# Gated FFN with linear attention: the last chunk of the down projection by seven products, another order of the second half's chunks, and one weight split behind an elu

## The chip, the cores and the metric

The kernel runs on one core of one Trainium2 chip. The metric is the device time of one execution in microseconds (us), as the median of several runs. A profile of one execution gives, for each engine, which instruction ran when. The engines are PE (TensorE, the matmuls; PEld is its weight load), DVE (VectorE), ACT (ScalarE), POOL (GpSimd) and SP (SyncE, which issues all DMAs here). Each engine works through its own list of instructions in order, and an instruction waits at its head until what it needs is done.

## The reference

```python
def reference(A_x, A_wqkv, A_wo, B_x, B_w1, B_b1, B_w2, B_b2):
    def _A_ref(x, wqkv, wo):            # 32 heads of 18, S = 2048, D = 576
        ...
        phi = lambda t: jnp.where(t > 0, t + 1, jnp.exp(t)) + 1e-6
        pq, pk = phi(q), phi(k)
        kv = jnp.einsum("bhsd,bhse->bhde", pk, v)
        z = jnp.einsum("bhsd->bhd", pk)
        num = jnp.einsum("bhqd,bhde->bhqe", pq, kv)
        den = jnp.einsum("bhqd,bhd->bhq", pq, z)[..., None] + 1e-6
        o = num / den
        return (lambda x, *d: x.transpose(*d))(o, 0, 2, 1, 3).reshape(B, S, D) @ wo
    def _B_ref(x, w1, b1, w2, b2):      # F = 4608
        h = jnp.einsum("bsd,df->bsf", x, w1) + b1
        h = _gelu(h)
        return jnp.einsum("bsf,fd->bsd", h, w2) + b2
    x = A_x
    xn = _layernorm(x, axis=-1)
    s = _A_ref(xn, A_wqkv, A_wo)
    g = _silu(_B_ref(xn, B_w1, B_b1, B_w2, B_b2))
    return x + s * g
```

## The kernel before, in words

All arithmetic is fp32. A matmul operand is split into a high part (ACT rounds it, a CAST) and a low part (DVE subtracts the high part from the value); a product takes three matmuls, high·high, high·low and low·high. In the rows of the profile the names end in `_h` and `_l`, and line L837 is the high part (`set_hi`), L840 the low part (`set_lo`).

There are three stages. In the first (to about 145 us) 16 tiles of 128 tokens are normalized and give keys and values. In the second (to about 279 us) the loop `for i in range(1, NT + 4)` at L1108 projects the queries (`query`, L317), applies the elu (`phi`: three ACT steps L330, L332, L334 and one DVE step L336, which writes `phiq`), divides by the sums (`normalize`), transposes (`transpose_p`) and multiplies (`attend`, L813) with `kw`, the output weight folded with the attention state. `kw` has five parts. `split_kw(k)` makes the high and low halves of part k (ACT L359, DVE L360), and `attend(0)` is the first to use them, part 0 to part 4 in turn. The result s goes to `s_dram`.

The third stage is the FFN. It runs over two halves of 1024 tokens, and in each half over NC = 9 chunks of 512 hidden features: 18 chunks, `step` in the code. A chunk has two `Up` (each two blocks of 128 features times two blocks of 512 tokens, by seven products of sums of blocks instead of eight plain ones, L1189) and then the down projection, also by seven products (`product`, L1351), in the order `ORDER = (1, 2, 7, 4, 5, 3, 6)`. A down product has two halves (`q2`) of 12 matmuls of 128x288, each into a PSUM tile `pm`, and one DVE add (L1357) puts each half into the accumulators `macc`: C11, C12, C21, C22 (two blocks of tokens, b, times two halves of the output's columns, n) and U1, a sum that three of them share and that `combine` (L1367) adds at the end.

The down products need sums of the gelu's outputs `g`: POOL makes them (`HOps.S`: number 7 L1317, 5 L1308, 6 L1311, 3 L1314, each for the pair `pr` = 0 and 1 of the two `Up`), then come `hi` and `lo`. `W1` and `W2` are the weights' operands, made in the first half and stored to DRAM (`w1_dram`, `w2_dram`); in the second half they are loaded back. Chunk 8's W2 operands are not stored.

What stands where is written out by hand. A chunk has 28 steps: after each of the 14 up products (steps 0 to 13) and after each half of a down product (14 to 27) `at_step` emits what the tables `PH`, `PW2`, `W2_NEXT` and others put there. `in_order` then fixes the order on PE, DVE, ACT and POOL as it is emitted; the DMAs on SP are put in order by a scheduler.

The last chunk (`plain`, step 17) is different. Its down projection is done plainly: `down_plain` (L1451) takes eight tiles of 128 tokens one after the other, each with 24 matmuls of 128x288 (the last tile in two pieces of 384 and 192 columns). A tile ends with a DVE add of the accumulator (L1462), the silu on ACT (L1463), a DVE multiply with s (L1420), an add of x (L1421) and the DMA to `out` (L1422). The first half's output is finished in the course of the second half (`finish`, L1439 and L1440 on POOL).

Of the kernel before, what the change touches and what calls it, by code (L numbers as in the profile page):

```python
# [8 lines left out]
F32 = mybir.dt.float32  # L9
# [29 lines left out]
NWARM = 20  # L39

# [4 lines left out]
def linear_attention_gated_ffn(ctx, tc, x, xT, wqkv, wo, w1, w1e, b1, w2, b2, out):  # L45
# [78 lines left out]
    w1_dram, w2_dram = {}, {}  # L124

# [512 lines left out]
    def load_w2_raw(n):  # L638
        raw = w2rp.tile([P, 4, CF // 2, HD], F32, tag="w2raw", name=f"w2raw{n}")
        nc.sync.dma_start(raw.rearrange("p b a d -> p (b a d)"), w2[n % NC])  # L640
        return raw
# [207 lines left out]
    def load_we(n):  # L849
# [3 lines left out]
        g, q = divmod(n % NP, WG)  # L853
# [8 lines left out]
    class W1:  # L862


        def __init__(self, n):
            self.n = n
            raw = stage_w1(f"w1raw{n}")
            nc.sync.dma_start(raw, w1[n % NP])
# [43 lines left out]
    class W1Loaded(W1):  # L912


        def __init__(self, n):
            self.n, self.tiles = n, {}
            for i in ("a", "c", "d"):
                if i == "c":
                    t = w1r.tile([P, 8, P], F32R, tag="stw", name=f"wc_{n}")
                else:  # L920
                    t = w1_tile(i, n)
                self.tiles[i] = t
                nc.sync.dma_start(t.bitcast(F32), w1_dram[n % NP, i])

    def load_six(n):

        t = w1_tile("e", n)
        for k in range(2):
            six[n + k] = t[:, 4 * k : 4 * k + 4]
            nc.sync.dma_start(six[n + k].bitcast(F32), w1_dram[(n + k) % NP, 6])  # L930
# [177 lines left out]
    for i in range(1, NT + 4):  # L1108
# [25 lines left out]
        if 1 < i < NT:  # L1134
            phi_query(i)
        if 2 <= i < NT + 2:
# [3 lines left out]
        for k in {2: (0,), 3: (2, 4)}.get(i, ()):  # L1140
# [30 lines left out]
    class Up:  # L1171
        late = []

        def __init__(self, n, w, xs):
            self.p, self.w = n % NP, w
# [36 lines left out]
        def step(self, i):  # L1212
# [12 lines left out]
            elif i == 6:  # L1225
                self.mm(A, 6, first=False)
                nc.scalar.copy(u1_sb, A)  # L1227
                if self.p:
                    self.gelu(0, 0, B)
            elif i == 5:  # L1230
                self.mm(E, 5)
                nc.scalar.copy(m5_sb, E)
                if not self.p:
# [16 lines left out]
    class W2:  # L1250
# [21 lines left out]
        def plain(self, f):  # L1272
            k = 2 - 2 * (f % 2)
            self.src["p", f] = self.raw[:, k : k + 2, f // 2]

        def hi(self, i):
            tag = ORDER[i[1]] if isinstance(i, tuple) else i
            self.tiles[i], self.ops[i] = op_tile(fr, [2, HD], f"w2_{tag}", 1, f"w2_{self.n}_")
# [7 lines left out]
        def load(self, i):  # L1286
            t, self.ops[i] = op_tile(fr, [2, HD], f"w2_{i}", 1, f"w2_{self.n}_")
            nc.sync.dma_start(t.bitcast(F32), w2_dram[self.n % NC, i])

    class HOps:  # L1290
# [28 lines left out]
        def hi(self, i, pr):  # L1319
            self.ops[i, pr] = hi_lo(gp, [P, 512], f"h{HBUF[i, pr]}", 1, f"h{i}{pr}_")  # L1320
# [12 lines left out]
    }  # L1333
    ORDER = (1, 2, 7, 4, 5, 3, 6)
    CHAIN = {2: 1, 3: 5, 4: 7}
# [36 lines left out]
    tails = {}  # L1372

    def load_xs(t):
        F = lambda v: v.bitcast(F32)
        flat = lambda v: F(v).rearrange("p a b -> p (a b)")[:, :D]
        if t == 0:
            xt, s_t = flat(w1_tile("a", "x0")), stage_w1("s0")[:, :D]
        elif t == 1:
            xt = flat(w1_tile("a", "x1"))  # L1380
            s_t = flat(w1p.tile([P, WB, P], F32R, tag="we", name="s1", bufs=2))
        elif t == 2:
            xt, s_t = (flat(w1_tile("a", f"{v}2")) for v in "xs")
        elif t == 3:
            xt, s_t = stage_w1("x3")[:, :D], flat(w1_tile("a", "s3"))
        elif t == 4:
            raw = F(fr.tile([P, 2, D], F32R, tag="w2_5", name="xs4", bufs=1))
            xt, s_t = raw[:, 0], raw[:, 1]
        else:
            if t == 5:  # L1390
                tails["h"] = F(x_hi(2, "xs56")).rearrange("p a b -> p (a b)")
                tails["l"] = F(x_lo(2, "xs7")).rearrange("p a b -> p (a b)")
            v = {5: tails["h"], 6: tails["h"][:, 2 * D :], 7: tails["l"]}[t]
            xt, s_t = v[:, :D], v[:, D : 2 * D]
        nc.sync.dma_start(xt, x[t * P : (t + 1) * P, :])
        nc.sync.dma_start(s_t, s_dram[t])
        tails["xs", t] = xt, s_t

    def tail_split(b, f):
        src = h.A[f // 2, b, f % 2]  # L1400
        if b == 0:
            pair = hi_lo(gp, [P, 512], f"h{f}", 1, f"hp{f}_")
        else:
            k = f % 2
            if f < 2 and ("t", 0) not in tails:
                tails["t", 0] = x_lo(0, "hp0")
            if f >= 2 and ("t", 1) not in tails:
                tails["t", 1] = x_lo(1, "hp1")
            t = tails["t", f // 2]
            pair = t[:, 2 * k, :], t[:, 2 * k + 1, :]  # L1410
        set_hi(pair, src)
        tails["hs", b, f] = pair, src

    def tail_lo(b, f):
        pair, src = tails["hs", b, f]
        set_lo(pair, src, nc.vector)

    def gate(t, c, xt, s_t, cs=slice(0, D), eng=nc.vector):

        nc.vector.tensor_tensor(s_t[:, cs], c[:, cs], s_t[:, cs], op=MUL)  # L1420
        eng.tensor_tensor(s_t[:, cs], s_t[:, cs], xt[:, cs], op=ADD)  # L1421
        nc.sync.dma_start(out[t * P : (t + 1) * P, cs], s_t[:, cs])  # L1422


# [26 lines left out]
    def down_plain(t, ws):  # L1451

        bi, q = divmod(t, QH)
        cs = slice(q * P, (q + 1) * P)
        seq = []
        for f, (wh, wl) in enumerate(ws):
            hh, hl = tails["hs", bi, f][0]
            seq += [(hh, wh), (hh, wl), (hl, wh)]
        dst = c_tile(bi, q).rearrange("p n d -> p (n d)")

        def end(ps, c):
            nc.vector.tensor_tensor(c, ps, c, op=ADD)  # L1462
            nc.scalar.activation(c, c, AF.Silu)  # L1463

        def mm(ps, w, i):
            st, w_all = seq[i]
# [252 lines left out]
```

## Time and profile before

| | us |
|---|---|
| median of 3 runs | 1092.71 (1092.48 to 1092.85) |
| the profiled execution: time | 1092.45 |
| its span in the trace | 1090.6 |
| outside the span | 1.85 |
| PE busy | 1082.6 (99%) |
| DVE, ACT, POOL busy | 798.2, 549.2, 454.6 |
| down products of one chunk (PE) | 22.39 |
| plain down projection of the last chunk (PE) | 25.71, from 1060.17 |

The span is from the first to the last event on the core, and the time is measured around it. A row of the timeline reads: start, duration, engine, line, operation, output<-inputs, number of instructions, and in brackets how long the engine was idle before it and for whom.

### The profile page before, as it was taken

Reading aid. Unit: us, or ns where it says so; the run is one execution under the profiler, and the core shown is the slowest. Engines: PE = TensorE matmul, PEld = TensorE weight load, DVE = VectorE, ACT = ScalarE, POOL = GpSimd, SP = SyncE. Lnnn points to the kernel's source line nnn. Section 1 sums busy time; section 2 is a strip of 40 time slices with the busy share of each in tenths; the row PEclk is TensorE's granted clock in tenths of the full one; section 3 lists DMA queues with packets and bytes.
Section 4 is the critical chain, followed back from the end, with each engine's and each line's share of the span. In section 5 each row is a group of like instructions: output and inputs, shape, how many; then the busy total and the mean of one; then the engine's idle time right before and its main releaser. Section 6 shows DMA issues by size and latency. Waiting matters only on the chain.

```text
span 1090.6 us, 18119 instructions
## 1 busy us (share of the span) xinstructions
PE 1082.6 (99%) x6704; PEld 1007.4 (92%) x6704; DVE 798.2 (73%) x1099; ACT 549.2 (50%) x956; POOL 454.6 (42%) x391
## 2 busy tenths in 40 slices
PE   9999999999999999999999999999999999999998
PEld 8999999999898998988989989899898998988988
DVE  7776559888688898888988988657475574664856
ACT  6545476455646456465564654624335244252552
POOL 3555414332547455464555553414325143341340
PEclk9999999999999999999999999999999999999999
DMA  7999635675958659576595669968676666767452
GB/s 239 239 222 214 212 105 192 213 246 183 343 222 316 219 192 334 170 294 237 204 330 181 258 235 408 379 233 308 224 232 214 211 228 223 231 219 222 132 184 87
DMA packets 87266, 254.58 MB, mean 233 GB/s; under 512 B 11783, under 2 KB 24071, under 8 KB 84490
## 3 DMA queue, kind: packets, MB, share of 16 engines
q1 hardware_dynamic: 87178, 253.42, 69.7%
q8 instruction: 53, 0.87, 0.3%
q14 instruction: 35, 0.29, 0.1%
HBM read 156.57 MB, written 94.58 MB: 230 GB/s over the span
## 4 chain that ended last, share of the span: by engine, by line
PE 98%; DVE 1%; SPq 0%; ACT 0%; DMA 0%; issue 0%; POOL 0%; POOLq 0%
PE pm L1351 35%; PE a L1189 16%; PE bc L1189 10%; PE e L1189 10%; PE pk L317 6%; PE ps_s L813 5%; PE pq L317 5%; PE pv L317 4%; PE pd L1467 2%; PE ps_kva L378 1%; PE ptp L795 1%; PE warm L365 0%; PE ps_kw L728 0%; PE ps_kvb L378 0%; DMA wa_rest0q<-xh 0%; SPq L963 0%
## 5 line engine op out<-in xcount | busy, mean ns | idle before, releaser
L1357 DVE TENSOR_TENSOR macc<-pm,macc 128x576 f32<-128x576 f32 x218 | 164.4, 754 | 55.5 <-PE pm L1351 54.9
L837 ACT CAST h_h<-g 128x512 fp32r<-128x512 f32 x204 | 122.6, 620 | 132.2 <-PE pm L1351 131.6
L840 DVE TENSOR_TENSOR h_l<-g,h_h 128x512 fp32r<-128x512 f32 x204 | 154.6, 769 | 14.9 <-ACT h_h L837 13.9
L1317 POOL TENSOR_TENSOR mid<-g 128x512 f32<-128x512 f32 x34 | 44.0, 1293 | 134.9 <-ACT g L1205 134.9
L1218 ACT COPY mid<-a 128x512 f32<-128x512 f32 x36 | 21.1, 587 | 110.3 <-PE a L1189 110.1
L1224 DVE TENSOR_TENSOR bc<-bc,mid 128x512 f32<-128x512 f32 x36 | 25.1, 698 | 51.5 <-PE bc L1189 40.7
L1311 POOL TENSOR_TENSOR g<-g 128x512 f32<-128x512 f32 x34 | 52.2, 1535 | 20.8 <-ACT h_h L837 16.7
L883 POOL TENSOR_TENSOR w1raw<-w1raw 128x256 f32<-128x256 f32 x18 | 13.3, 737 | 113.9 <-ACT h_h L837 65.3
L1237 DVE TENSOR_TENSOR z<-a,mid 128x512 f32<-128x512 f32 x36 | 25.1, 698 | 46.6 <-PE a L1189 46.6
L1439 POOL TENSOR_TENSOR fin1l<-fin1h,fin1l 128x288 f32<-128x288 f32 x8 | 6.5, 808 | 122.8 <-DMA fin1l<-s_dram 57.9
L1314 POOL TENSOR_TENSOR g<-g 128x512 f32<-128x512 f32 x34 | 52.6, 1546 | 7.6 <-DVE h_l L840 5.5
L1308 POOL TENSOR_TENSOR g<-g 128x512 f32<-128x512 f32 x34 | 50.3, 1481 | 2.7
L778 POOL TENSOR_TENSOR pbuf<-phiq,den 128x576 f32<-128x576 f32 x16 | 19.0, 1188 | 61.2 <-DVE den L777 57.8
L1227 ACT COPY mid<-a 128x512 f32<-128x512 f32 x36 | 21.2, 588 | 44.3 <-PE a L1189 44.3
L1238 ACT COPY mid<-a 128x512 f32<-128x512 f32 x36 | 21.1, 587 | 40.0 <-DVE z L1237 40.0
L840 DVE TENSOR_TENSOR h_l<-mid,h_h 128x512 fp32r<-128x512 f32 x34 | 38.0, 1118 | 2.4 <-ACT h_h L837 2.4
L317 PE MATMUL pk<-wkv_h,xh 128*128 128x288 f32 (+1 forms) x160 | 38.2, 321 | 0.5 <-DVE xh L245 0.5
L317 PE MATMUL pk<-wkv_l,xh 128*128 128x288 f32 (+1 forms) x160 | 38.3, 322 | 0.1
L317 PE MATMUL pq<-wq_h,xh 128*128 128x288 f32 x160 | 34.7, 298 | 0.7 <-DVE phiq L336 0.7
L813 PE MATMUL ps_s<-kw_h,th 128*128 128x288 f32 x160 | 35.2, 302 | 0.0
L765 POOL TENSOR_TENSOR eq<-phiq,zb 128x576 f32<-128x576 f32 x16 | 22.9, 1432 | 27.6 <-DMA zb<-z_dram 19.4
L317 PE MATMUL pq<-wq_l,xh 128*128 128x288 f32 x160 | 34.3, 296 | 0.0
(891 smaller groups left out, 3709.0 us busy)
## 6 DMA issues: line engine op xcount, KB each, us to landing
we<-we_dram SPq DMA_DIRECT2D x36, 448.0 KB, 5.7
w2raw<-w SPq DMA_DIRECT2D x10, 1152.0 KB
w1raw<-w SPq DMA_DIRECT2D x18, 512.0 KB, 4.8
op_a<-wa SPq DMA_DIRECT2D x18, 512.0 KB, 4.6
op_c<-wc SPq DMA_DIRECT2D x18, 512.0 KB, 4.2
op_d<-wd SPq DMA_DIRECT2D x18, 512.0 KB, 2.7
wc<-op_c SPq DMA_DIRECT2D x18, 512.0 KB, 4.6
wa<-op_a SPq DMA_DIRECT2D x18, 512.0 KB, 5.0
```

What stands on the lines that cost most here:

```text
L317: nc.tensor.matmul(ps[:, h, : ws.stop - ws.start], st, w[:, k, ws], start=(begin and i == 0), stop=(end and i == len(seq) - 1), skip_group ...
L813: nc.tensor.matmul(ps[:, h, :HD], st[:, k, :], w[:, k, h * HD : (h + 1) * HD], start=(i == 0), stop=(i == len(seq) - 1),)
L837: nc.scalar.copy(pair[0], src)
L840: eng.tensor_tensor(pair[1], src, pair[0].bitcast(F32), op=SUB)
L1189: nc.tensor.matmul(ps, st, mv, start=first and n == 0, stop=n == len(seq) - 1, skip_group_check=True,)
L1224: tt(B, B, m1_sb, op=ADD)
L1308: tt(src[5, pr], A(1, 0), A(1, 1), op=ADD)
L1311: tt(src[6, pr], src[5, pr], A(0, 0), op=SUB)
L1314: tt(src[3, pr], A(0, 1), src[6, pr], op=SUB)
L1317: tt(src[7, pr], A(0, 0), A(1, 0), op=SUB)
L1351: nc.tensor.matmul(ps[:, q, :HD], hs[p][st][:, cs], m[:, p, :], start=(n == 0 and i not in CHAIN), stop=(n == 5), skip_group_check=True,)
L1357: nc.vector.tensor_tensor(dst, src, dst, op=ADD)
```

## The change

There are three parts.

1. **The last chunk.** `down_plain` and what belongs to it are gone. `last_chunk` does the seven products in the order `LAST = (1, 2, 5, 3, 6, 7, 4)`. Product 1 stays in the PSUM tiles `a0`, `a1`, and 6, 7 and 4 are added onto it there; product 2 goes to `e`, then 5, and 3 onto 5. After each half `drain` brings the accumulators in: after 2 the block C11 is final, after 6 C12, after 7 C22, after 4 C21. Each final block goes through `gate`: silu on ACT, multiply by s and add of x, then the DMA to `out`. For product 2 POOL does multiply and add; for 6, 7 and the first half of 4 DVE multiplies and POOL adds; the last half of 4 is done in two pieces of 128x288, multiply and add on DVE. The sums and splits of the operands stand in the table `PL`, their buffers in `HLAST`; the three `combine` stand at steps 1 to 3 instead of 4.
2. **The order of the second half's chunks.** They were taken 0 to 8; now `AGAIN` takes 8, 0, 1, ..., 7. The first one finds its W2 operands still in place, so the loads of W2 at the change of halves are gone; the last one (now chunk 7) loads its seven W2 operands like the others, where chunk 8's raw W2 was loaded and split before.
3. **The fifth split.** `split_kw(4)` moves from i = 3, between the splits 2 and 3, to i = 4, behind `phi_query(4)`.

The first place is DVE in the last chunk. The rows before are those of the plain tiles (`pd`; `xs`, `wa_s` and so on hold x and s):

```order
L1462 TENSOR_TENSOR macc<-pd_11579,macc 128x576
L1420 TENSOR_TENSOR xs_11327<-macc,xs_11327 128x576
L1421 TENSOR_TENSOR xs_11327<-xs_11327 128x576
L1462 TENSOR_TENSOR macc<-pd_11609,macc 128x576
L1420 TENSOR_TENSOR xs_11427<-macc,xs_11427 128x576
L1421 TENSOR_TENSOR xs_11427<-xs_11427 128x576
```

Now, from the first half of product 6 on (L1470 is the add in `drain`, L1442 the multiply by s, L847 the low part of an operand, L1474 the add of product 4):

```order
L1470 TENSOR_TENSOR e_11467<-a_11431,macc 128x2x288
L1442 TENSOR_TENSOR gated_11366<-e_11467,gated_11366 128x2x288
L847 TENSOR_TENSOR h_l<-g,h_h 128x512
L1470 TENSOR_TENSOR e_11468<-a_11432,macc 128x288
L1470 TENSOR_TENSOR e_11468<-a_11433,macc 128x288
L1442 TENSOR_TENSOR gated_11382<-e_11468,gated_11382 128x2x288
L1470 TENSOR_TENSOR e_11467<-a_11431,macc 128x2x288
L1442 TENSOR_TENSOR gated_11428<-e_11467,gated_11428 128x2x288
```

Each multiply stands between the add of its own half and the add of the next; the silu between them is on ACT.

The second place is ACT at the end of the last `Up`. Before, after the last gelu come the last splits and then only silus:

```order
L1205 ACTIVATE g<-bc_11345,b1c 128x512
L837 CAST hp_11454<-g 128x512 x2
L1463 ACT_TABLE_LOAD
L1463 ACTIVATE macc<-macc 128x576 x7
L1463 ACTIVATE macc<-macc 128x384
```

Now (L1440 is the silu, L844 a high part; `h_x_11487` are the operands 5 and 3 of pair 1):

```order
L1214 ACTIVATE g<-bc_11324,b1c 128x512
L844 CAST wa_h_11425<-g 128x512
L1440 ACT_TABLE_LOAD
L1440 ACTIVATE macc<-macc 128x2x288
L844 CAST h_x_11487<-g 128x512
L1440 ACTIVATE macc<-macc 128x2x288
L844 CAST h_x_11507<-mid 128x512
L844 CAST h_x_11487<-g 128x512
```

The high parts of the operands 5 and 3 (pair 1) stand behind the silus of product 2's two halves; on POOL the sum for operand 3 stands likewise behind the multiply and add of product 2's first half.

The third place is DVE around the elu of tile 4. Before (`kr_1804`, `kr_1840`, `kr_1822` are the parts 2, 4 and 3):

```order
L360 TENSOR_TENSOR kw_l<-kr_1804,kw_h 128x576
L360 TENSOR_TENSOR kw_l<-kr_1840,kw_h 128x576
L360 TENSOR_TENSOR kw_l<-kr_1822,kw_h 128x576
L773 TENSOR_REDUCE den_1943<-eq_1911 128x32
L776 TENSOR_SCALAR den_1943<-den_1943 128x32
L777 RECIPROCAL den_1943<-den_1943 128x32
L336 SCALAR_TENSOR_TENSOR phiq_1982<-pq_1948,eq_1978 128x576
```

Now:

```order
L367 TENSOR_TENSOR kw_l<-kr_1804,kw_h 128x576
L367 TENSOR_TENSOR kw_l<-kr_1822,kw_h 128x576
L780 TENSOR_REDUCE den_1941<-eq_1911 128x32
L783 TENSOR_SCALAR den_1941<-den_1941 128x32
L784 RECIPROCAL den_1941<-den_1941 128x32
L343 SCALAR_TENSOR_TENSOR phiq_1980<-pq_1946,eq_1976 128x576
L367 TENSOR_TENSOR kw_l<-kr_1840,kw_h 128x576
```

Part 4 of `kw_l` now follows `phiq`; on ACT its high part follows the elu's third step in the same way.

The diff, cut to its core:

```diff
+AGAIN = (NC - 1, *range(NC - 1))
...
+    def chunk_of(step):
+        return step if step < NC else AGAIN[step - NC]
+
+    def pair_of(n):
+        return 2 * chunk_of(n // 2) + n % 2
...
-                nc.sync.dma_start(t.bitcast(F32), w1_dram[n % NP, i])
+                nc.sync.dma_start(t.bitcast(F32), w1_dram[pair_of(n), i])
...
+        if i == 4:
+            split_kw(4, nc.vector)
...
-        for k in {2: (0,), 3: (2, 4)}.get(i, ()):
+        for k in {2: (0,), 3: (2,)}.get(i, ()):
             split_kw(k, nc.vector)
...
-            nc.sync.dma_start(t.bitcast(F32), w2_dram[self.n % NC, i])
+            nc.sync.dma_start(t.bitcast(F32), w2_dram[chunk_of(self.n), i])
...
+    HLAST = {
+        (1, 0): 0, (1, 1): 1, (2, 0): 2, (2, 1): 3, (6, 0): 4, (4, 1): 0, (5, 0): "w", (3, 0): "w",
+        (5, 1): (0, 0), (3, 1): (0, 2), (6, 1): (1, 0), (7, 1): (1, 2), (7, 0): (3, 0), (4, 0): (3, 2),
+    }
+    LAST = (1, 2, 5, 3, 6, 7, 4)
...
+    def load_gated(k):
+        flat = x_hi((0, 2, 1, 3)[k], f"gated{k}").bitcast(F32).rearrange("p a b -> p (a b)")
+        xt, st = (flat[:, v : v + 2 * D].rearrange("p (q d) -> p q d", q=2) for v in (0, 2 * D))
...
+    def last_chunk(hops, ws, base):
+        a0 = bank2("a0")[:, :, :HD]
+        a1 = [bank1(f"a1{q}")[:, :HD] for q in range(2)]
+        e = []
+        tt = nc.vector.tensor_tensor
+        def gate(b, n, q2, c, q=slice(0, 2), eng=(nc.vector, nc.gpsimd), last=False):
+            cs = slice(n * HD, (n + 1) * HD)
+            xt, st = (v[:, q, cs] for v in gated[2 * b + q2 // 2])
             nc.scalar.activation(c, c, AF.Silu)
+            to = c if last else st
+            eng[0].tensor_tensor(to, c, st, op=MUL)
+            eng[1].tensor_tensor(st, to, xt, op=ADD)
...
+        def drain(i, q2):
...
+            if i == 1:
+                for a, c, _ in banks(C11):
+                    tt(c, a, c, op=ADD)
+            elif i in (2, 5, 3):
+                c = macc[:, q2 : q2 + 2, {2: C11, 5: C22, 3: C12}[i], :]
+                tt(c, ps, c, op=ADD)
+                if i == 2:
+                    gate(0, 0, q2, c, eng=(nc.gpsimd, nc.gpsimd))
+            elif i in (6, 7):
+                for a, c, to in banks({6: C12, 7: C22}[i]):
+                    tt(to, a, c, op=ADD)
+                gate(int(i == 7), 1, q2, ps)
+            else:
+                for q, (a, c, _) in enumerate(banks(C21)):
+                    tt(a, a, c, op=ADD)
+                    if q2:
+                        gate(1, 0, q2, a, q=q, eng=(nc.vector, nc.vector), last=True)
+                    else:
+                        gate(1, 0, q2, a)
+        for k, i in enumerate(LAST):
...
+            for q2 in (0, 2):
...
+                        nc.tensor.matmul(
+                            ps, hs[p][st][:, cs], m[:, p, :], start=n == 0 and i in (1, 2, 5),
...
+                drain(i, q2)
+                at_step(base + 14 + 2 * k + q2 // 2)
...
+    PL = dict(
+        S={(7, 0): 7, (5, 0): 8, (6, 0): 9, (3, 0): 10, (7, 1): 13, (5, 1): 14, (6, 1): 15, (3, 1): 16},
+        hi={
+            (1, 0): 7, (2, 0): 8, (5, 0): 9, (6, 0): 10, (1, 1): 11, (2, 1): 12, (3, 0): 13,
+            (5, 1): 16, (7, 0): 17, (3, 1): 18, (6, 1): 19, (7, 1): 20, (4, 0): 21, (4, 1): 22,
+        },
...
+            if change:
+                w2t[step + 1] = w2t[step]
+            else:
                 make(W2, w2t, step + 1)
                 for i, at in W2_NEXT.items():
-                    add(base + at + 10 * change, lambda i=i, n=step + 1: w2t[n].load(i))
...
+                    add(base + at, lambda i=i, n=step + 1: w2t[n].load(i))
...
+            for k, m in enumerate((C12, C21, C22)):
+                add(base + 1 + k, combine, m, nc.gpsimd)
+            for k, at in enumerate((9, 10, 13, 14)):
+                add(base + at, load_gated, k)
...
-    for t in range(2 * QH):
-        down_plain(t, ws)
```

More of the change, by code (lines that the diff above doesn't have):

```diff
@@ L1227, in step @@
                 nc.scalar.copy(u1_sb, A)
-                if self.p:
+                if not self.first:
                     self.gelu(0, 0, B)
@@ L1232, in step @@
                 nc.scalar.copy(m5_sb, E)
-                if not self.p:
+                if self.first:
                     self.gelu(0, 0, B)
@@ L1370, in c_tile @@
         return macc[:, q, 2 * bi : 2 * bi + 2, :]
[L1372 to L1422, printed above, removed]
     def silu_first(s):
@@ L1624, in linear_attention_gated_ffn @@
                     add(base + 26 + k, combine, C21, nc.gpsimd, slice(2 * k, 2 * k + 2))
-            for what in ("S", "hi", "lo"):
-                for (i, pr), at in PH[what].items():
-                    add(base + at, getattr(h, what), i, pr)
+        for what in ("S", "hi", "lo"):
+            for (i, pr), at in (PL if plain else PH)[what].items():
+                add(base + at, getattr(h, what), i, pr)
         if half == 1 and c == 0:
@@ L1660, in linear_attention_gated_ffn @@
         if plain:
+            last_chunk(h.ops, w2t[step].ops, base)
             break
```

121 lines of the change are left out of this document (55 added, 66 removed).

## The prediction

> **What bounds the kernel now.** I read the page first, then the chain of waits in order of time, then PE's own waits, and only then the timeline of the end.
>
> ```profile
> span 1090.6 us, 18119 instructions
> PE 1082.6 (99%) x6704; PEld 1007.4 (92%) x6704; DVE 798.2 (73%) x1099; ACT 549.2 (50%) x956; POOL 454.6 (42%) x391
> ```
>
> ```profile
> 1015.53 22.39 PE pm L1351 x168
> 1037.91 1.62 PE a L1189 x7
> 1060.17 25.71 PE pd L1467 x192
> ```
>
> ```profile
> PE warm L365 <- POOL ident masks.py:199: 2.0, 1, 2.0
> PE pq L317 <- DVE phiq L336: 0.7, 1, 0.7
> PE pk L317 <- DVE xh L245: 0.5, 1, 0.5
> ```
>
> PE is the bound, and it waits for 3.2 us in the whole span. So a change can gain in three ways: fewer matmuls, PE's last wait (0.7 us for `phiq`), or what follows the last matmul. A down projection by seven products takes 22.39 us of PE for 168 matmuls, so 1.60 us for a half of 12; the last, plain one takes 25.71. A chunk is 44.64 us (1015.53 to 1060.17), and none of the waits lies in the FFN, the change of halves included. The end of the program, on DVE and on ACT:
>
> ```profile
> 1082.51 0.76 DVE L1462 TENSOR_TENSOR macc<-pd,macc 128x576 f32<-128x576 f32 x1
> 1084.01 0.76 DVE L1420 TENSOR_TENSOR xs<-macc,xs 128x576 f32<-128x576 f32 x1 [0.75 <-ACT macc L1463]
> 1084.69 0.55 DVE L1462 TENSOR_TENSOR macc<-pd,macc 128x384 f32<-128x384 f32 x1
> ```
>
> ```profile
> 1087.63 0.36 DVE L1421 TENSOR_TENSOR xs<-xs 128x192 f32<-128x192 f32 x1
> ```
>
> ```profile
> 1083.30 0.68 ACT L1463 ACTIVATE macc<-macc 128x576 f32<-128x576 f32 x1 [2.49 <-DVE macc L1462]
> 1085.27 0.53 ACT L1463 ACTIVATE macc<-macc 128x384 f32<-128x384 f32 x1 [1.29 <-DVE macc L1462]
> 1086.30 0.36 ACT L1463 ACTIVATE macc<-macc 128x192 f32<-128x192 f32 x1 [0.49 <-DVE macc L1462]
> ```
>
> Two things are to be seen. PE's matmuls end at 1085.88, DVE's last add at 1087.99, and the output's DMA takes the other 2.6 us to 1090.6. And one round on DVE, add, wait of 0.75 for the silu, multiply, takes 2.18 us from the start of an add (1082.51) to the start of the next instruction behind the multiply (1084.69). Plain tiles come every 3.2 us, so the round fits under PE.
>
> **Part 1, the last chunk.** On PE it removes 25.71 us and adds 22.39: a gain of 3.3 us if PE doesn't wait and the tail stays as it is. Neither holds, because the outputs become final in the last three products, every 1.60 us, and DVE has a round of 2.18 for each. DVE is in order, and each multiply stands ahead of the next half's add. The rows for the walk, of DVE, ACT and POOL in the last chunk and of groups over the span:
>
> ```profile
> 1060.31 0.69 DVE L1242 TENSOR_TENSOR bc<-bc,mid 128x512 f32<-128x512 f32 x1
> 1061.05 0.69 DVE L840 TENSOR_TENSOR hp_l<-g,hp_h 128x512 fp32r<-128x512 f32 x1
> ```
>
> ```profile
> 1061.04 0.69 ACT L1205 ACTIVATE g<-bc,b1c 128x512 f32<-128x512 f32 x1
> ...
> 1062.77 1.28 ACT L1463 ACT_TABLE_LOAD   x1
> ```
>
> ```profile
> 1045.56 7.96 POOL L1367 TENSOR_TENSOR macc<-macc 128x1152 f32<-128x1152 f32 x3
> 1084.90 1.41 POOL L1421 TENSOR_TENSOR xs<-xs 128x576 f32<-128x576 f32 x1 [31.38 <-DVE xs L1420]
> ```
>
> ```profile
> L837 ACT CAST h_h<-g 128x512 fp32r<-128x512 f32 x204 | 122.6, 620 | 132.2 <-PE pm L1351 131.6
> L840 DVE TENSOR_TENSOR h_l<-g,h_h 128x512 fp32r<-128x512 f32 x204 | 154.6, 769 | 14.9 <-ACT h_h L837 13.9
> L1317 POOL TENSOR_TENSOR mid<-g 128x512 f32<-128x512 f32 x34 | 44.0, 1293 | 134.9 <-ACT g L1205 134.9
> L1308 POOL TENSOR_TENSOR g<-g 128x512 f32<-128x512 f32 x34 | 50.3, 1481 | 2.7
> L330 ACT ACTIVATE eq<-pq 128x576 f32<-128x576 f32 x16 | 10.4, 652 | 34.3 <-PE pq L317 34.3
> ```
>
> The `combine`s (8 us of POOL) move ahead of `finish` and end near 1046.7; the first sum waits for a gelu four us later, so this costs nothing. Product 1 starts at 1060.17 as the plain one did. The last gelu ends at 1061.73, and POOL's sums for pair 1 (1.29, then 1.48 to 1.5 each) end at 1063.0, 1064.5 and 1066.0. Product 2's first half ends at 1060.17 + 3 x 1.60 = 1064.97. Then come the add (to 1065.77), the silu (0.69, to 1066.50; the table load fits in before), the cast of operand 5 that stands behind it (to 1067.05) and its low part on DVE (0.69, to 1067.78). Product 5 starts at 1066.57 and needs that low part with its sixth matmul at 1067.24: PE waits 0.57.
>
> Next on DVE are product 2's second add (to 1068.46) and the low part of operand 7, whose cast stands behind the second silu: 1069.78 to 1070.46. The add of product 5's first half comes only after it, to 1071.15. Product 3 accumulates onto the same tile and would have started at 1070.34: PE waits 0.85. On POOL the multiply and add of product 2's first half (1.41 each, from 1066.54) push the sum for operand 3 to 1070.8; cast and low part end at 1072.2, and the sixth matmul of product 3 wants them at 1071.86: 0.38 more. So PE loses 1.80 us, and product 6's first half ends at 1060.17 + 9 x 1.60 + 1.80 = 1076.37.
>
> From there DVE is the bound. Three rounds with one add take 0.80 + 0.69 + 0.69 = 2.18 each. (The silu now reads PSUM: 0.65, as the relu from PSUM in L330.) Two rounds whose add is in two 288-column pieces (0.455 each, between the 0.36 of 192 columns and the 0.55 of 384) take 2.25. With the low part of operand 4 in between (0.61) that is 11.65 us, against 8.0 of PE for the same five halves; PE now waits for DVE, since product 4 accumulates onto the tile that product 7's add must have read. The last two pieces, each add, silu, multiply and add in turn on 288 columns (0.45 + 0.04 + 0.41 + 0.04 + 0.45 + 0.03 + 0.38 = 1.80), do not overlap on DVE: 3.60 us. DVE ends at 1076.41 + 11.65 + 3.60 + 0.07 = 1091.73, that is 3.74 later than the 1087.99 of before. SP's last stores wait in order behind POOL's add for product 4's first half, which ends near 1089.6 and so holds nothing. The last DMA has 144 KB instead of 96; I add 0.1 us.
>
> [...]
>
> Bounds. The PE waits are worth at most -1.8 us if all vanish. POOL at 1.33 for 576 columns (half of one of L1367's 1152-column adds) or at 1.67 (L1308's 1.48 for 512 columns, scaled) instead of 1.41 moves the end by -0.2 or +0.6, in the same walk. Low parts at their mean of 0.77 instead of 0.69, which is with other engines at work, add 0.2, and rows longer still up to 1. Rounds 0.12 shorter (add and multiply at the 0.69 of the 512-column add L1242) take 0.6 off. Loads of x and s (eight before, four pairs now) start when the x operands are last read, 1052 to 1060, and the first is wanted at 1066.5; a 288 KB load took 3.2 us (row below), so this has cover of several us.
>
> **Part 2, the chunks' order.** PE waits nowhere around the change of halves, and each operand is loaded most of a chunk ahead of its use, so I cost it at 0. Seven loads of W2 go from SP's queue at the change of halves and come back before the last chunk, where other chunks have them too. One thing is new: the load of a W1 operand now needs a store that stands just ahead of it.
>
> ```profile
> 636.48 0.32 SPq L834 DMA_DIRECT2D op_c<-wc  x1
> 637.75 0.32 SPq L834 DMA_DIRECT2D op_d<-wd  x1
> 638.16 0.41 SPq L923 DMA_DIRECT2D wc<-op_c  x1
> 639.61 0.32 SPq L834 DMA_DIRECT2D op_a<-wa  x1
> 643.15 0.32 SPq L834 DMA_DIRECT2D op<-w  x1
> ```
>
> ```profile
> op_c<-wc SPq DMA_DIRECT2D x18, 512.0 KB, 4.2
> ```
>
> ```profile
> wa_x<-x SPq DMA_DIRECT2D x2, 288.0 KB, 3.2
> ```
>
> With 4.2 us for such a store to land, SP would stand until about 641 at that load, and the store after it be 1 to 2 us late; by the next one at 643.15 SP has caught up. The operand is wanted tens of us later. Bounds: 0 to +3.
>
> **Part 3, the fifth split.**
>
> ```profile
> 173.74 0.43 PE L813 MATMUL ps_s<-kw_l,th 128*128 128x288 f32 x2
> 174.88 0.53 PE L317 MATMUL pq<-wq_h,xh 128*128 128x288 f32 x2 [0.71 <-DVE phiq L336]
> ```
>
> ```profile
> 172.73 0.78 ACT L334 ACTIVATE eq<-eq,tiny 128x576 f32<-128x576 f32 x1
> ```
>
> ```profile
> L360 DVE TENSOR_TENSOR kw_l<-kr,kw_h x4: 695/746/1117, 167.7 to 172.0; 128x576 fp32r<-128x576 f32 x4
> ```
>
> ```profile
> 174.07 0.76 DVE L336 SCALAR_TENSOR_TENSOR phiq<-pq,eq 128x576 f32<-128x576 f32 x1
> ```
>
> Without one split ahead of it `phiq` starts about 0.7 us earlier, 173.36 to 174.12, and the 0.71 us that PE waited are gone. But `attend(0)` ends with the fifth part, and PE wants its low half at 173.74. It now comes behind `phiq`: 174.12 to 174.80. Its two matmuls (0.27) start at 174.84, and the next query at 175.11 instead of 174.88: +0.2. Ends: -0.71 if nothing takes the wait's place, +0.6 with the longest of the split's rows (1.12).
>
> **Sum.** 3.74 + 0.1 + 0 + 0.2 = +4.05 on 1092.45, the profiled execution: 1096.5. The median of the runs is 0.26 above that execution, so 1096.8.
>
> **Rivals.** (B) DVE keeps pace and PE stays the bound: the products end at 1060.17 + 22.39 = 1082.56, and with 2.7 us of DVE tail and 2.7 of DMA the span is 1088.0, 2.6 less: 1090.1. For it speaks that PE really has 3.3 us less to do; it decides if a round gets under 1.60 us, which needs the 0.75 of waiting for the silu out of DVE's list. The order of the rows forbids it. (C) The early waits vanish, because sums and splits come in time; then DVE's rounds start at 1074.6 and the end is 1.8 earlier: 1095.0. Against it, DVE has little free between 1069.8 and 1076 in the walk. (D) POOL and low parts go at their slow values, all rounds start a microsecond or two later: 1098.2. (E) The split's part does what it takes away, -0.7 instead of +0.2: 1095.9, inside the range. (F) The W1 load holds PE at the change of halves: 1099.8 at its end of +3; PE's cover speaks against it.
>
> **How the numbers follow.** About 0.2% (2.2 us) is what a measurement of this kernel can tell from no change. Chances: the forecast with E 0.60 (1095.5 to 1098), C 0.15, D 0.17, B 0.04, F 0.04. Slower by over 2.2 us means over 1094.9: the forecast, D and F nearly whole and half of C, 0.85. Within 2.2: 0.11, the rest of C and the forecast's low corner, where C and E and shorter rounds meet. Faster: 0.04, B. The range 1094.2 to 1098.9 leaves out B, F and the edge of D.
>
> **What would show it.** In the profile after: PE's products from 1060.4 on with waits of about 0.6 before the sixth matmul of product 5, about 0.9 and 0.4 at product 3, and then waits on DVE at products 7 and 4; DVE adds from product 6 on 2.2 us apart with a wait of about 0.7 on ACT ahead of each multiply; about 6 us from the last matmul to DVE's last add, instead of 2.1; chunks at 44.64 us across the change of halves; PE's wait near 174 us now on `kw_l`, not `phiq`. I am wrong if PE ends later than DVE's list lets me think (rounds under 1.7 us), or if the DVE rounds begin before 1075.

## The result, and the profile after

The changed kernel takes 1099.35 us (median of 4 runs, 1098.81 to 1099.44) where the kernel before takes 1092.70 (4 runs): a ratio of 1.006, 95% interval 1.0043 to 1.0077. That is 6.65 us slower. I had forecast slower, by 4.1 us, with 1098.9 as the upper end of the range, so the direction was right and the size was not. The profiled execution after took 1098.81 us, its span is 1097.1 (before 1092.45 and 1090.6).

The head of the page and PE's waits after (columns of the second fence: who waited for whom, total us, times, the longest):

```profile
span 1097.1 us, 18090 instructions
PE 1080.7 (99%) x6680; PEld 1003.9 (92%) x6680; DVE 798.3 (73%) x1102; ACT 549.4 (50%) x958; POOL 480.8 (44%) x407
```

```profile
PE ps_s L820 <- DVE kw_l L367: 1.3, 1, 1.3
PE e L1494 <- DVE h_x L847: 1.2, 2, 1.0
PE a L1494 <- DVE e L1470: 1.0, 1, 1.0
PE e L1494 <- DVE macc L1465: 1.0, 1, 1.0
```

PE works 1.9 us less and waits 4.5 us at places where it waited 0.7 before. The chain of waits puts the last full chunk here:

```profile
1016.42 22.39 PE pm L1371 x168
```

With 44.64 us for a chunk the last one starts at 1061.06 (before 1060.17). Its DVE, from the low part of operand 5 (pair 1) on, with the places that the prediction walked through:

```profile
1067.90 1.50 DVE L847 TENSOR_TENSOR h_x<-g,h_x 128x512 fp32r<-128x512 f32 x1 [1.26 <-ACT h_x L844]
1069.32 0.74 DVE L1465 TENSOR_TENSOR macc<-e,macc 128x576 f32<-128x576 f32 x1
1071.33 1.15 DVE L847 TENSOR_TENSOR h_x<-mid,h_x 128x512 fp32r<-128x512 f32 x1 [1.26 <-ACT h_x L844]
1072.41 0.74 DVE L1465 TENSOR_TENSOR macc<-e,macc 128x576 f32<-128x576 f32 x1
1073.07 1.23 DVE L847 TENSOR_TENSOR h_x<-g,h_x 128x512 fp32r<-128x512 f32 x1
...
1074.89 1.24 DVE L847 TENSOR_TENSOR h_x<-g,h_x 128x512 fp32r<-128x512 f32 x1
...
1076.73 0.67 DVE L847 TENSOR_TENSOR h_x<-mid,h_x 128x512 fp32r<-128x512 f32 x1
...
1078.76 0.77 DVE L1470 TENSOR_TENSOR e<-a,macc 128x576 f32<-128x576 f32 x1
1080.23 0.76 DVE L1442 TENSOR_TENSOR gated<-e,gated 128x576 f32<-128x576 f32 x1 [0.70 <-ACT e L1440]
...
1090.64 0.46 DVE L1474 TENSOR_TENSOR a<-a,macc 128x288 f32<-128x288 f32 x1
...
1093.84 0.46 DVE L1443 TENSOR_TENSOR gated<-a,gated 128x288 f32<-128x288 f32 x1
```

Two things are to be seen. The DVE rounds begin at 1078.76, 17.70 us after the chunk's start, and the forecast's walk has 16.24. And a low part (L847) takes 0.67 in one row and 1.15 to 1.50 in four others of the same shape, while the adds between them, which read PSUM, keep to 0.74 to 0.77. The four long rows are the low parts of operands 5 (pair 1), 7 (pair 0), 3 and 6 (pair 1). POOL in that stretch:

```profile
1067.44 1.41 POOL L1442 TENSOR_TENSOR gated<-macc,gated 128x576 f32<-128x576 f32 x1 [0.47 <-ACT macc L1440]
1068.93 1.75 POOL L1443 TENSOR_TENSOR gated<-gated 128x576 f32<-128x576 f32 x1
1070.64 1.29 POOL L1318 TENSOR_TENSOR g<-g 128x512 f32<-128x512 f32 x1
1071.89 1.87 POOL L1442 TENSOR_TENSOR gated<-macc,gated 128x576 f32<-128x576 f32 x1
1073.83 1.76 POOL L1443 TENSOR_TENSOR gated<-gated 128x576 f32<-128x576 f32 x1
```

Put the ends side by side. POOL's operations end at 1068.85, 1071.93, 1073.76 and 1075.59; the four long low parts end at 1069.40, 1072.48, 1074.30 and 1076.13: 0.55, 0.55, 0.54 and 0.54 later. So these low parts, begun while POOL worked, were not slowed a little, they stood until POOL's operation was over. In turn POOL's 1.75 at 1068.93 ends 1.28 after the low part that was running (1069.40). So the two took turns.

The whole difference in spans, term by term (measured by rows shown here or in the next section):

| term | forecast | measured |
|---|---|---|
| fifth split | +0.2 | +0.76 |
| order of the chunks | 0 | 0 |
| last chunk's start to the first round on DVE | 16.24 | 17.70 |
| five rounds with one low part (1078.76 to 1090.64) | 11.65 | 11.88 |
| last two pieces (1090.64 to 1094.30) | 3.67 | 3.66 |
| DVE's end to the span's end | 2.7 | 2.8 |

The misses are 0.56, 1.46, 0.23 and 0.1; with 0.13 by which the last chunk starts later beyond the split (+0.89 against +0.76) they make the 2.5 us between +4.05 and +6.5. What makes the 0.13 was not tried; the order of the chunks does not (see its run below).

### The profile page after: what moved, and what is told of

It is laid out like the page before. It is cut to its first block, busy times and chain, and to the rows that moved or that the text cites. A ratio compares the mean times of both kernels' runs of the same rounds, so it can differ in the third digit from the quotient of the medians.

```text
span 1097.1 us, 18090 instructions
## 1 busy us (share of the span) xinstructions
PE 1080.7 (99%) x6680; PEld 1003.9 (92%) x6680; DVE 798.3 (73%) x1102; ACT 549.4 (50%) x958; POOL 480.8 (44%) x407
## 4 chain that ended last, share of the span: by engine, by line
PE 95%; DVE 2%; ACT 1%; SPq 1%; DMA 1%; issue 0%; DVEq 0%; ACTq 0%
PE pm L1371 35%; PE a L1198 16%; PE e L1198 10%; PE bc L1198 10%; PE pk L324 6%; PE ps_s L820 5%; PE pq L324 5%; PE pv L324 4%; PE ps_kva L385 1%; PE ptp L802 1%; DMA w<-wqkv 0%; PE a L1494 0%; PE e L1494 0%; SPq L970 0%; PE ps_kw L735 0%
## 5 line engine op out<-in xcount | busy, mean ns | idle before, releaser
L844 ACT CAST h_h<-g 128x512 fp32r<-128x512 f32 x210 | 126.2, 620 | 134.3 <-PE pm L1371 133.0
L847 DVE TENSOR_TENSOR h_l<-g,h_h 128x512 fp32r<-128x512 f32 x210 | 160.6, 775 | 14.9 <-ACT h_h L844 13.9
L1321 POOL TENSOR_TENSOR mid<-g 128x512 f32<-128x512 f32 x36 | 46.6, 1294 | 139.8 <-ACT g L1214 139.8
L1315 POOL TENSOR_TENSOR g<-g 128x512 f32<-128x512 f32 x36 | 55.2, 1534 | 20.9 <-ACT h_h L844 16.7
L1318 POOL TENSOR_TENSOR g<-g 128x512 f32<-128x512 f32 x36 | 55.5, 1542 | 7.7 <-DVE h_l L847 5.6
L1312 POOL TENSOR_TENSOR g<-g 128x512 f32<-128x512 f32 x36 | 53.6, 1490 | 2.8
L847 DVE TENSOR_TENSOR h_l<-mid,h_h 128x512 fp32r<-128x512 f32 x34 | 38.2, 1123 | 2.2 <-ACT h_h L844 2.2
L820 PE MATMUL ps_s<-kw_l,th 128*128 128x288 f32 x160 | 34.4, 296 | 1.3 <-DVE kw_l L367 1.3
```

The lines of the kernel that those rows point to most:

```text
L820: nc.tensor.matmul(ps[:, h, :HD], st[:, k, :], w[:, k, h * HD : (h + 1) * HD], start=(i == 0), stop=(i == len(seq) - 1),)
L844: nc.scalar.copy(pair[0], src)
L847: eng.tensor_tensor(pair[1], src, pair[0].bitcast(F32), op=SUB)
L1312: tt(src[5, pr], A(1, 0), A(1, 1), op=ADD)
L1315: tt(src[6, pr], src[5, pr], A(0, 0), op=SUB)
L1318: tt(src[3, pr], A(0, 1), src[6, pr], op=SUB)
```

## The experiments

There are two theories. A: a DVE operation with both operands in SBUF (a low part) stands while POOL works; this is the 1.46 us and the larger price of the split. B: those rows are long for another reason (where their tiles lie, what DMAs run). A third question is what the rounds on DVE are worth. All times below are medians beside runs of the kernel before on the same chip (1092.80 in the first four, 1092.58 in the others). As the kernel before itself differs by 0.2 there, differences of that size between medians of different rows say nothing. "From the chunk's start" means from the start of its last full down projection in the chain of waits plus 44.64 us:

| kernel | median us | chunk's start | to first round | to DVE's end | to the span's end |
|---|---|---|---|---|---|
| before | 1092.70 | 1060.17 | none | 27.82 | 30.43 |
| changed | 1099.35 | 1061.06 | 17.70 | 33.24 | 36.04 |
| split back | 1098.30 | 1060.53 | 17.72 | 33.26 | 36.07 |
| old order | 1099.74 | 1062.13 | 17.72 | 33.26 | 36.27 |
| late gates | 1099.05 | 1061.44 | 16.23 | 31.77 | 35.56 |
| pipelined | 1096.51 | 1061.35 | 17.72 | 29.78 | 33.65 |
| table | 1097.03 | 1061.02 | 16.31 | 31.23 | 34.08 |
| all together | 1092.48 | 1060.49 | 16.33 | 26.77 | 30.41 |

The starts differ by the first stage too (tenths of a microsecond from run to run, 1.1 in the profiled run of the old order), so the tail is read from the chunk's start.

**The split put back in the changed kernel.**

```diff
-        if i == 4:
-            split_kw(4, nc.vector)
-        for k in {2: (0,), 3: (2,)}.get(i, ()):
+        for k in {2: (0,), 3: (2, 4)}.get(i, ()):
```

> The changed kernel with one part undone: the fifth split of the folded weight stands again with the third, ahead of the elu's phiq. Theory A (the moved split costs more than I forecast, because the part's low half is written 0.5 us slower while POOL works on the pbuf operand): PE's wait on kw_l near 175 us goes from 1.3 to the 0.7 on phiq that the kernel before had, the last chunk's products start near 1060.2 instead of 1061.06, and the time falls by 0.87 us, 1099.35 to 1098.5. The price in my prediction: 0.2 us less. If the 0.89 us later start of the last chunk comes from somewhere else, the last chunk still starts near 1061.

Measured: 1098.30 (1097.83 to 1098.68), 1.05 less than the changed kernel. **The split alone, moved in the kernel before**, is the same edit the other way:

> The kernel before with only the fifth split moved behind the elu. Theory A: +0.87 us, near 1093.6, with a PE wait of 1.3 us on kw_l near 175 us and the low half of that split at about 1.2 us on DVE beside POOL's pbuf. The price in my prediction: +0.2 us, 1092.9, low half at 0.68.

Measured: 1093.40, 0.6 more than before (ratio 1.0007, interval 0.9998 to 1.0015, so the time by itself is not told from no change). The traces give the size without the spread of the starts. From the chain of waits, the last stretch ahead of the elu and the first full one behind it: before, then changed, then with the split back.

```profile
149.81 4.58 PE pq L317 x34
...
179.42 3.71 PE ps_s L813 x28
```

```profile
149.63 4.58 PE pq L324 x34
...
180.00 3.71 PE ps_s L820 x28
```

```profile
150.02 4.58 PE pq L324 x34
...
179.63 3.71 PE ps_s L820 x28
```

29.61 us before, 30.37 changed, 29.61 with the split back, and with the split alone 30.37 again (149.60 to 179.97): the split costs 0.76. In the kernel with the split alone:

```profile
173.33 1.17 POOL L778 TENSOR_TENSOR pbuf<-phiq,den 128x576 f32<-128x576 f32 x1 [2.72 <-DVE den L777]
173.86 1.24 DVE L360 TENSOR_TENSOR kw_l<-kr,kw_h 128x576 fp32r<-128x576 f32 x1
...
175.16 0.53 PE L813 MATMUL ps_s<-kw_l,th 128*128 128x288 f32 x2 [1.29 <-DVE kw_l L360]
```

`phiq` came earlier, as forecast. But so did the reciprocal `den` ahead of it (172.80 instead of 173.68), and by its bracket `den` released POOL's `pbuf`, at 173.33 instead of 174.21. The split that now stands behind `phiq` begins in the middle of `pbuf` and ends at 175.10, 0.60 after POOL's 174.50. PE's wait is 1.29 where it was 0.71.

**The old order of the chunks.**

```diff
-AGAIN = (NC - 1, *range(NC - 1))
+AGAIN = tuple(range(NC))
...
-            if self.n < NC - 1:
+            if self.n < NC:
...
-            if change:
-                w2t[step + 1] = w2t[step]
-            else:
+            if True:
...
-                    add(base + at, lambda i=i, n=step + 1: w2t[n].load(i))
+                    add(base + at + 10 * change, lambda i=i, n=step + 1: w2t[n].load(i))
```

> The changed kernel with the second half's chunks in ascending order again, so that seven W2 loads stand in the last chunk and none at the change of halves (all of W2's chunks are stored and loaded). The prediction and theory A: no change, 1099.35 within 0.3 us, the last chunk starts near 1061.06 and ends 36.0 us later. Rival: the other order costs, or these loads in the last chunk hurt the operands' loads there: the time moves by 0.5 us or more.

Measured: 1099.74 (1099.23 to 1100.1), 0.39 more, with intervals that overlap. PE's waits are those of the changed kernel and the last chunk runs as before to 0.02 us up to DVE's end. In the chain, from the start of the first full down projection to that of the last, the changed kernel takes 714.67 us (301.75 to 1016.42) and this one 714.66 (302.83 to 1017.49). So the order costs nothing, as forecast; the later start of this run comes from the first stage.

**POOL's gates of product 2 late.** The multiply and add on POOL for product 2 are emitted behind the adds of product 6, so that POOL has nothing to do while DVE makes most of the low parts:

```diff
+            if eng[0] is nc.gpsimd and not now:
+                late.append(lambda: gate(b, n, q2, c, eng=eng, now=True))
+                return
...
                 drain(i, q2)
+                if i == 6:
+                    late.pop(0)()
```

> The changed kernel with POOL's multiply and add for the two halves of product 2 issued only after product 6's halves are drained, so that POOL is idle while DVE makes the low parts of operands 7, 3 and 6 (pairs 0 and 1). Theory A (a low part on DVE, both operands in SBUF, takes 1.1 to 1.5 us instead of 0.68 because POOL works beside it): those low parts go back to about 0.68, the first DVE round of product 6 starts 1.3 us earlier against the last chunk's start, 16.4 us after it instead of 17.7, and the time falls by 1.3 us, to 1098.0. Rival B (the low parts are long there for another reason, such as where their tiles lie or what DMAs run): they stay at 1.15 to 1.5, the rounds start where they did, and the time stays within 0.3 us of 1099.35.

Measured: 1099.05 (1098.6 to 1099.52), 0.3 less; the time alone would speak for B. The trace does not. DVE, the same four low parts, the first round and the end, and POOL's rows:

```profile
1068.29 0.97 DVE L847 TENSOR_TENSOR h_x<-g,h_x 128x512 fp32r<-128x512 f32 x1 [1.26 <-ACT h_x L844]
...
1071.19 0.69 DVE L847 TENSOR_TENSOR h_x<-mid,h_x 128x512 fp32r<-128x512 f32 x1 [1.26 <-ACT h_x L844]
...
1072.46 0.68 DVE L847 TENSOR_TENSOR h_x<-g,h_x 128x512 fp32r<-128x512 f32 x1
...
1073.73 0.68 DVE L847 TENSOR_TENSOR h_x<-g,h_x 128x512 fp32r<-128x512 f32 x1
...
1077.67 0.77 DVE L1474 TENSOR_TENSOR e<-a,macc 128x576 f32<-128x576 f32 x1 [0.23 <-PE a L1498]
...
1092.75 0.46 DVE L1447 TENSOR_TENSOR gated<-a,gated 128x288 f32<-128x288 f32 x1
```

```profile
1067.43 1.28 POOL L1318 TENSOR_TENSOR g<-g 128x512 f32<-128x512 f32 x1
1080.03 1.74 POOL L1447 TENSOR_TENSOR gated<-gated 128x576 f32<-128x576 f32 x1 [11.32 <-DVE gated L1446]
...
1087.48 5.47 POOL L1447 TENSOR_TENSOR gated<-gated 128x576 f32<-128x576 f32 x4
```

The three low parts that now meet no POOL work take 0.68 to 0.69; the one that still meets POOL's sum for operand 3 (1067.43 to 1068.71) ends at 1069.26, 0.55 later. The rounds start 16.23 us after the chunk's start, 1.47 earlier, where the forecast had them (16.24). So A holds. That the total is met to 0.01 us is partly luck: one low part still stands here, and with the gates gone operand 3's sum no longer waits behind them, for which the forecast had 0.38. In the changed kernel that sum was not what counted, since DVE reached operand 3's low part at 1073.07 without waiting for it. My price for the whole run did not hold: I had counted the 1.3 us through to the end. DVE does end 1.47 us earlier from the chunk's start, but POOL, with four operations shifted behind 1080, is busy up to 1092.95, and its last 288 KB store leaves together with DVE's last two. The span ends 3.8 us after DVE's last operation instead of 2.8. That the stores crowd each other there is read from these ends, it was not tried by itself.

**POOL kept busy in the kernel before.**

```diff
             ps = bank2(f"pd{t}")
+            if 0 < t < 5:
+                for _ in range(2):
+                    nc.gpsimd.tensor_tensor(mid[:, 3], mid[:, 3], mid[:, 4], op=SUB)
```

> The kernel before with two extra POOL operations of 128x512 (both operands in SBUF, on a scratch tile, their result is not used) for each of the last chunk's tiles 1 to 4, so that POOL is busy while DVE works there. Nothing else is changed. Theory A: DVE's tensor-tensor operations with both operands in SBUF in these tiles grow from 0.76 to between 1.0 and 1.5 us each, those with one operand in PSUM stay at 0.76, and POOL's operations take longer than 1.29 where they meet them. Rival B (the low parts' tiles or their DMAs make them slow): all stay at 0.76. The time itself may grow by some us; it is not what the run is for.

Measured: 1093.85 (one run). The place was missed: POOL waits for nothing there and ran its eight operations from 1053.74 on (1.64 us each on average), ahead of the tiles' multiplies, which stay at 0.76. It met the low parts of the last `Up` instead, the very operations in question, with no other change to their tiles or loads:

```profile
1053.74 13.69 POOL L1476 TENSOR_TENSOR mid<-mid 128x512 f32<-128x512 f32 x8
```

The line of the low parts in this stretch (count, then ns: least, median, most), first before, then with POOL busy, and last two adds with an operand in PSUM in the run with POOL busy:

```profile
L840 DVE TENSOR_TENSOR hp<-g,hp x4: 681/689/693, 1056.6 to 1062.9; 128x512 fp32r<-128x512 f32 x4
L840 DVE TENSOR_TENSOR hp_l<-g,hp_h x2: 692/692/693, 1059.7 to 1061.0; 128x512 fp32r<-128x512 f32 x2
```

```profile
L840 DVE TENSOR_TENSOR hp<-g,hp x4: 720/1358/1777, 1057.0 to 1064.5; 128x512 fp32r<-128x512 f32 x4
L840 DVE TENSOR_TENSOR hp_l<-g,hp_h x3: 1052/1182/1785, 1054.3 to 1061.7; 128x512 fp32r<-128x512 f32 x3
```

```profile
L1246 DVE TENSOR_TENSOR e<-e,mid 128x512 f32<-128x512 f32 x1 | 0.7, 687 | 0.0
L1242 DVE TENSOR_TENSOR bc<-bc,mid 128x512 f32<-128x512 f32 x1 | 0.7, 687 | 0.0
```

Nothing of the computation is touched, and the low parts go from 0.69 to between 0.72 and 1.79 while the PSUM adds stay at 0.69. So theory B does not explain these rows.

**The multiplies behind the next half's add.** The closing multiply of a half is held back until DVE has done the next half's add:

```diff
+            if eng[0] is nc.gpsimd:
+                close()
             else:
+                held.append(close)
...
                     tt(to, a, c, op=ADD)
+                while held:
+                    held.pop(0)()
                 gate(int(i == 7), 1, q2, ps)
```

> The changed kernel with one edit in DVE's order: the multiply that closes a half comes only after the add of the next half, so that DVE does not stand through the silu (0.70 us) in each round. If the serial rounds of add, silu and multiply are what makes the tail long, as the prediction has it: the waits of 0.70 ahead of each multiply go, a round takes about 1.4 to 1.7 us instead of 2.1 to 2.45, the rounds still start 17.7 us after the last chunk's start, DVE ends 3.7 to 4.1 us earlier, near 1090.4, and POOL's last add and its 288 KB store end the span at about 1094: a time of 1096.2, 3.1 us less. Rival: PE's products, not DVE's rounds, set the end by then (PE's last matmul at 1087.9): less than 1.5 us is gained.

Measured: 1096.51 (1096.16 to 1096.71), 2.84 less than the changed kernel. DVE, one full round and the end:

```profile
1083.45 0.77 DVE L1477 TENSOR_TENSOR e<-a,macc 128x576 f32<-128x576 f32 x1
1084.13 0.75 DVE L1444 TENSOR_TENSOR gated<-e,gated 128x576 f32<-128x576 f32 x1
1084.98 1.04 DVE L1477 TENSOR_TENSOR e<-a,macc 128x288 f32<-128x288 f32 x2
...
1090.67 0.46 DVE L1445 TENSOR_TENSOR gated<-a,gated 128x288 f32<-128x288 f32 x1
```

The waits of 0.70 are gone, a round takes 1.53 (1083.45 to 1084.98), and DVE ends 29.78 us after the chunk's start instead of 33.24: 3.46 less. The rounds start where they did (17.72). So the forecast's picture of the tail, serial rounds on DVE, is shown by taking it away. The span gains 2.4 of the 3.46 from the chunk's start; here too the last stores of POOL and DVE leave together, and the end comes 3.87 us after DVE's last operation.

**The table of the last chunk's operands.**

```diff
-        S={(7, 0): 7, (5, 0): 8, (6, 0): 9, (3, 0): 10, (7, 1): 13, (5, 1): 14, (6, 1): 15, (3, 1): 16},
+        S={(7, 0): 7, (5, 0): 8, (6, 0): 9, (3, 0): 10, (7, 1): 13, (5, 1): 14, (6, 1): 15, (3, 1): 15},
...
-            (5, 1): 16, (7, 0): 17, (3, 1): 18, (6, 1): 19, (7, 1): 20, (4, 0): 21, (4, 1): 22,
+            (5, 1): 15, (3, 1): 17, (6, 1): 18, (7, 1): 19, (7, 0): 19, (4, 0): 20, (4, 1): 21,
...
-            set_lo(self.ops[i, pr], self.src[i, pr], nc.vector)
+            eng = nc.gpsimd if i == 4 and self.c == n_chunks - 1 else nc.vector
+            set_lo(self.ops[i, pr], self.src[i, pr], eng)
```

(The second change is of `hi`; `lo` has the same with (5, 1) at 16.)

> The changed kernel with only the table of the last chunk's operands altered: the sum for operand 3 one step earlier, ahead of POOL's gates of product 2, the cast of operand 5's second half ahead of product 2's first silu on ACT, the cast and low part of operand 7's first half two steps later, operand 4's two low parts on POOL. If PE's early waits and DVE's crowded list before the rounds cost 1.5 us beyond my forecast: PE's waits in products 5 and 3 fall from 2.2 to below 1.2 us, the rounds start 1.3 to 1.7 us earlier against the last chunk's start (16.0 to 16.4 instead of 17.7) and the time falls by 1.5 to 2.7 us, to 1096.6 to 1097.8. Rival: the work only moves about on DVE and POOL, the rounds start as late, no change.

Measured: 1097.03 (1096.77 to 1097.14), 2.32 less. PE's waits in products 5 and 3:

```profile
PE e L1495 <- DVE macc L1466: 0.7, 1, 0.7
```

From 2.2 us to 0.7; the rounds start 16.31 us after the chunk's start, and DVE ends 2.0 us earlier. 1.4 us of it are there at the first round, 0.6 come from the low part that no longer stands between the rounds. Those that are left on DVE still wait for POOL (0.96 at 1066.52, 1.11 at 1069.47, 1.23 at 1071.17, 3.08 for the two from 1072.99).

**All of it together**, with the split back, and POOL's last add and store in two pieces:

```diff
+                if b and not n and not last:
+                    for k in range(2):
+                        eng[1].tensor_tensor(st[:, k], to[:, k], xt[:, k], op=ADD)
+                        nc.sync.dma_start(out[(t + k) * P : (t + k + 1) * P, cs], st[:, k])
+                    return
```

> All edits that should help together: the pipelined multiplies, the altered table, the fifth split back in its old place, and product 4's first half added and stored on POOL in two pieces of 144 KB. Theory: 3.1 (pipelined) + 2.0 to 2.7 (table) + 0.75 (split) + up to 0.9 (two stores) less than the changed kernel's 1099.35, with what overlaps taken off: PE ends near 1084, DVE near 1087, span 1089.8, a time of 1091.5, 1.2 us below the kernel before. Rival: PE's early waits come back once DVE is quicker, or POOL's adds end it: 1093 or more, no gain over the kernel before.

Measured: 1092.48 (1092.11 to 1093.64, 11 runs) beside 1092.58: ratio 1.0, interval 0.9991 to 1.0009. No gain over the kernel before, and the rival's number was the better one.

```profile
1086.80 0.46 DVE L1450 TENSOR_TENSOR gated<-a,gated 128x288 f32<-128x288 f32 x1
```

DVE ends 1.05 us earlier from the chunk's start than in the kernel before (26.77 against 27.82), and the span's end comes 3.64 us after that instead of 2.6. So of the 3.3 us by which seven products are shorter on PE, 1.05 reach DVE's end and nothing reaches the end of the span, where the stores of POOL and DVE all leave in the last microseconds. That the stores cost this is read from these ends and not shown by a run of its own; whether their issue from SP or the DMA engines would be the limit stays open.

## Why the prediction was wrong, and where it was right

Right were the direction, the mechanism of the tail, and the order of the causes. Rounds with one add were forecast at 2.18 and measured 2.14 (1088.50 to 1090.64, the last of them):

```profile
1086.10 1.03 DVE L1470 TENSOR_TENSOR e<-a,macc 128x288 f32<-128x288 f32 x2
...
1088.50 0.76 DVE L1474 TENSOR_TENSOR a<-a,macc 128x576 f32<-128x576 f32 x1
```

Rounds with a two-piece add were 2.40 (1086.10 to 1088.50) and 2.47 instead of 2.25, because the second piece starts 0.57 after the first; less what the others were shorter, that is the 0.23 in the table. The last pieces (3.66 for 3.67), the order of the chunks (0) and PE's wait near 174 us, on `kw_l` and no longer on `phiq`, came as written. Of the waits forecast at products 7 and 4 one came, at product 4 (1.0 us). The multiplies that read PSUM took 0.76, as those from SBUF did.

Wrong was one duration, in two places: the low parts were priced as if nothing stood in their way. The walk has the low part of operand 5 at "0.69, to 1067.78", and likewise those of 7 and 3; I allowed 0.2 us more for "other engines at work" and "up to 1" for longer rows. But in the walk the POOL operations stand right beside those low parts (1.41 each, "from 1066.54"). The four rows are together 2.40 us longer than 4 x 0.68.

The step that failed is therefore "PE loses 1.80 us". The chain of waits after, from the sixth matmul of product 3 on:

```profile
1074.36 2.78 PE e L1494 x19
1077.14 1.60 PE a L1494 x12
...
1078.76 0.78 DVE e L1470
```

Nine halves of 1.60 from 1061.06 would end at 1075.46; product 6's first half ended at 1078.74, so PE lost 3.28, and PE still released the first round. (The brackets of PE's waits, 0.99, 0.97 and 0.23, add up to less: they count from the end of the row before, and PE's rows overlap: a matmul's row is 0.29 long and the next starts 0.13 after it started. The first matmul behind each of these waits is 0.40 long.) Before 1074.36 the chain runs through three of the four long low parts, those of operands 5, 7 and 3, which are 0.82, 0.47 and 0.55 longer than 0.68: 1.84 in all. The fourth fell into slack. With the walk's first two waits, 0.57 + 0.85 + 1.84 = 3.26. The walk's third wait, 0.38, was to be for operand 3's sum. A wait came there too, but for DVE's list, and it is contained in the 1.84: POOL's sum was done at 1071.93, before DVE got to that low part.

The split's step failed the same way: "174.12 to 174.80" assumed 0.68, and `pbuf`, which the earlier `den` releases, made it 1.24. My upper end of +0.6 took the longest of the split's rows, 1.12, without asking what ran beside it; 0.76 lies above it.

Of the rivals, (D), POOL and low parts at their slow values, named the right rows at 1098.2; it was too small, since it took a wait for a slower rate. (E), the split gaining 0.7, is refuted; (C) needed the early waits gone and they grew; (B) and (F) did not show.

The row that should have warned was on record in the prediction: 695, 746 and 1117 ns for one operation of one shape. Looking at what ran beside the 1117 would have given the cause: it began at 170.31, inside a POOL operation (169.39 to 170.82), and ended 0.61 us behind it.

## What to carry to other kernels

Before pricing a vector operation whose two tensor operands both lie in SBUF, look at what GpSimd does at that moment. In these traces it stood until the end of a GpSimd tensor-tensor operation that was already running, up to 1.1 us more for a 0.69 us operation, and the wait showed as a longer duration, not as idle time. With the GpSimd work moved three low parts took 0.68 to 0.69 (the late gates), but ask first what the moved work will end with. DVE operations of 128x576 with an operand in PSUM kept their 0.74 to 0.77 beside GpSimd; no run moved a low part's operand there. And where fewer matmuls bring the results in faster than an in-order engine can close them (here 1.60 us for a half on PE against rounds of 2.14 to 2.47 on DVE), put the next piece's add ahead of this piece's multiply before counting the matmuls as a gain; then count the stores that leave together: the span's end came 3.87 us after DVE's last operation in the pipelined run, 2.8 in the changed kernel, though the stores were not tried by themselves.

## What the runs showed of the hardware

Unexpected was how exact the taking of turns is. The rows of the seven traces with the changed last chunk have 42 low parts that end after 1058 us, stand alone in a row and begin during a POOL operation. All 42 end 0.54 to 0.56 us after that operation's end, whatever part of it was left (0.42 to 1.03 us). Low parts that met no POOL operation took 0.67 to 0.69. A POOL operation of 128x576 that began during such a low part ended 1.27 to 1.30 us after it. DVE operations of 128x576 with one operand in PSUM kept their 0.74 to 0.77 beside POOL. A multiply of 128x384 with both operands in SBUF (L1420) took 0.89 in the run with POOL busy, from 1087.35, and ended 0.42 us after POOL's add of 128x576 (1086.42 to 1087.82); in the kernel before it met only the last 0.13 us of that add and took 0.56 (from 1086.18).
